# Routing three of the four groups of tokens: one comparison and the splitting of the ranks, on VectorE before and on GpSimd after

## The chip, the cores and the metric

The kernel runs on one core of one Trainium2 chip. TensorE (PE, with its weight loads as PEld), VectorE (DVE), ScalarE (ACT), GpSimd (POOL) and SyncE (SP, which only issues DMAs here) run instruction queues of their own and wait for each other by semaphores. The metric is the device time of one execution in microseconds, lower is better.

## The reference

Linear attention is followed by a mixture of experts with one expert per token. `x` is the attention's output with one row of 512 values for each of 4608 tokens.

```python
def phi(x):
    proj = np.einsum('bhsd,df->bhsf', x, w_phi)
    proj = proj - np.max(np.abs(proj), axis=-1, keepdims=True)
    return np.concatenate([np.exp(proj), np.exp(-proj)], axis=-1)
q_p, k_p = (phi(q), phi(k))              # batch 8, heads 8, seq 576, dim 64, 128 features
kv = np.einsum('bhsf,bhsd->bhfd', k_p, v)
z = np.sum(k_p, axis=2)
num = np.einsum('bhsf,bhfd->bhsd', q_p, kv)
den = np.einsum('bhsf,bhf->bhs', q_p, z)[..., None] + 1e-06
attn = num / den
# mixture of experts: 8 experts, 512 -> 1024 -> 512
logits = x @ w_gate
expert_idx = np.argmax(logits, axis=1)
gate_w = softmax(logits)[np.arange(N), expert_idx]
for e in range(E):
    mask = expert_idx == e
    out[mask] = gate_w[mask, None] * (np.maximum(x[mask] @ w1[e], 0.0) @ w2[e])
```

## The kernel before

The attention works in 16 units: 4 groups of two batches, and in each group 4 pairs of heads. A unit takes its tokens in 9 chunks of 128. Products in fp32 are made from a high and a low part: ScalarE rounds (`xh`, `kh`, `vh`) and GpSimd or VectorE subtracts (`xl`, `kl`, `vl`). The steps of a unit are: `project` (three matmuls for each chunk into `ps_proj`, then VectorE's largest magnitude `mx` and the difference `t`), `k_features` and `k_parts` (exponentials `e`, then `kh` and `kl`), `q_features` (four transposes `pt` of `t`, then exponentials `qp`), the products `pk` of keys and values, `pf` (the folding with `w_gate`), and `pn`, which `normalize` turns into attention rows `xrow` and logits `lgc` (VectorE's `rec`, `rec`, `xrow`, `lgc`). `merge`, `zipped` and `ordered` weave the projections of one unit between the products of the last. `ps_proj` and `pt` have two buffers each, so that VectorE must have made `t` from one `ps_proj` before TensorE may use that buffer again, and TensorE's transposes wait for `t`.

The routing of a group (`route`) runs during the first unit pairs of the next group. Its steps are put between the products one at a time by `spread`. For the first three groups `final` is None, and there `X`, the engine of the small element-wise steps, is GpSimd. `logits`, `top` and `first_top` reduce on VectorE; `shift` and `candidates` are GpSimd's. `one_hot` compares the expert's number with each token's choice (`oh_b`), copies it to fp32 (`onehot`), and `sum_up` counts (`gsum` on VectorE, added to `base`). After some steps of pause, `count_ranks` counts with matmuls (`prk`) the place of each token among its expert's, `rank` reduces it to one number for each token, `rank_parts` splits it into a block of 128 and the place in it, and `rank_values` writes these as fp32, `blk` and `rkr`. Then `select` makes for each of 9 chunks one 128x128 table on VectorE (`sel_p`) and one on GpSimd (`sel_h`), and `gate`, `gate_sum`, `gate_store` make the gate weights (`se`, `gt`). The fourth group (`final` given) is routed at the end of the attention, with all of it on VectorE. The third pass is followed by `lead`, which fetches the first rows for the experts.

A scheduler sets the order on each engine from the order of the calls and from its own estimate of times, so that an edit in one step can move others. Each engine works strictly in that order. A wait of VectorE holds up all that stands behind it.

Of the kernel before, what the change touches and what calls it, by code (L numbers as in the profile page):

```python
# [14 lines left out]
ALU = mybir.AluOpType  # L15
AX = mybir.AxisListType
# [3 lines left out]
P = 128  # L20
# [8 lines left out]
NC = 9  # L29
# [12 lines left out]
W = 73  # L42
XW = DM + 4
BIG = 8192.0


@with_exitstack
def tile_linear_attention_moe(
# [12 lines left out]
    V, A, G, T = nc.vector, nc.scalar, nc.gpsimd, nc.tensor  # L61
# [98 lines left out]
    blk = rt.tile([P, NTILE], F32, name="blk")  # L160
# [410 lines left out]
    def route(g, lgc, c0, n, final=None):  # L571

        j0 = g * NC + c0
        js = slice(j0, j0 + n)
        r = {}
# [3 lines left out]
        X = V if final is not None else G  # L579

        def tile_of(name, shape, dtype=F32, **kw):
            r[name] = sg.tile(shape, dtype, name=name, **kw)[:, 0:n]
            return r[name]
# [22 lines left out]

        def one_hot():
            oh_b = tile_of("oh_b", [P, NC, E], BF16)
            V.tensor_tensor(
                oh_b,  # L610
                iota_em.unsqueeze(1).to_broadcast([P, n, E]),
                choice[:, js].unsqueeze(2).to_broadcast([P, n, E]),
                op=ALU.is_equal,
            )
            X.tensor_copy(onehot[:, js, :], oh_b)
            r["base_b"] = sg.tile([P, E], BF16, name="base_b")
            X.tensor_copy(r["base_b"], base)
# [26 lines left out]
                V.tensor_tensor(tile_of("rks", [P, NC, E]), prk, onehot[:, js, :], op=ALU.mult)  # L644

        def rank():
            with nc.allow_low_precision("ranks are integers"):
                V.tensor_reduce(tile_of("rki", [P, NC], I32), r["rks"], axis=AX.X, op=ALU.add)

        def rank_parts():  # L650
            rkb = tile_of("rkb", [P, NC], I32)
            V.tensor_single_scalar(rkb, r["rki"], 7, op=ALU.arith_shift_right)
            V.tensor_single_scalar(r["rki"], r["rki"], P - 1, op=ALU.bitwise_and)

        def rank_values():
            X.tensor_copy(blk[:, js], r["rkb"])
            X.tensor_copy(tile_of("rkr", [P, NC], bufs=2), r["rki"])

        def select_a(c):

# [27 lines left out]
        steps = [logits, top, shift, candidates, first_top, one_hot]  # L688
        selects = [lambda c=c: select(c) for c in range(n)]
        ranks = [rank, rank_parts, rank_values]  # L690
        gates = [gate, gate_sum, gate_store]
        if final is not None:
# [171 lines left out]
    def tokens_of():  # L864
# [6 lines left out]
        emp = sg.tile([P, NB], F32, name="emp")  # L871
        V.tensor_scalar(emp, pp, 0.5, BIG, op0=ALU.is_lt, op1=ALU.mult)
        V.scalar_tensor_tensor(sidx, pp, -1.0, emp, op0=ALU.add, op1=ALU.add)
# [200 lines left out]
    op = ctx.enter_context(tc.tile_pool(name="op", bufs=2, side="left", reuse_waits="tile"))  # L1074
# [142 lines left out]
```

## Time and profile before

| | |
|---|---|
| median of 3 runs | 940.46 us (940.34 to 940.65) |
| profiled execution, its own time | 942.13 us |
| its span in the profile | 940.1 us |
| TensorE, matmuls | busy 900.6 us, 96% |
| VectorE | busy 591.0 us, 63% |
| ScalarE | busy 591.9 us, 63% |
| GpSimd | busy 499.4 us, 53% |
| mean granted TensorE clock | 0.986 |

The span runs from the first to the last instruction in the profile; 2.0 us lie around it. Busy shares are averages over the whole span. The attention ends near 438 us and the experts fill the rest. The three routing passes that the change touches run near 134 to 162, 236 to 264 and 339 to 367 us.

### The profile page before, as it was taken

The numbers are of one execution on the slowest core, as the hardware profiler recorded it, in microseconds if no ns is written. First come the engines' busy times: TensorE is split into PE (matmuls) and PEld (weight loads), VectorE is DVE, ScalarE is ACT, GpSimd is POOL, SyncE is SP. The second block draws the span as 40 slices with busy tenths as digits, with TensorE's granted clock in tenths as the row PEclk, the third lists the DMA queues.
The fourth block names the chain that finished last, engine by engine and source line by source line (L and its number), as shares of the span: only waits on it lengthen the run. The fifth ranks groups of instructions, "written<-read, shape, count | busy, mean of one in ns | idle before, by whom it ended". The sixth has DMA issues, their size and how long they took to land. (4 is left out here: it accounts for less than half of the span.)

```text
span 940.1 us, 18395 instructions
## 1 busy us (share of the span) xinstructions
PE 900.6 (96%) x6824; PEld 844.2 (90%) x6824; DVE 591.0 (63%) x1016; ACT 591.9 (63%) x895; POOL 499.4 (53%) x355
## 2 busy tenths in 40 slices
PE   6999998999899999999999999999999999999995
PEld 5899998999899989998789999999999999987884
DVE  7767779777887778847864444444444444457850
ACT  5977776777677766654555555555555555568961
POOL 6666668666686669543443333333333333346641
PEclk9999999999999999997999999999999999999998
DMA  4333333333233333143044144441434634764100
GB/s 128 112 98 100 105 105 94 104 93 104 54 89 103 105 105 94 50 141 112 14 136 134 45 144 127 142 128 45 149 115 155 213 117 148 224 204 136 45 24 15
DMA packets 64348, 102.38 MB, mean 109 GB/s; under 512 B 10686, under 2 KB 28478, under 8 KB 64256
## 3 DMA queue, kind: packets, MB, share of 16 engines
q1 hardware_dynamic: 56928, 80.34, 27.6%
q0 software_dynamic: 6720, 20.80, 7.1%
q8 instruction: 54, 0.88, 0.4%
q14 instruction: 38, 0.31, 0.1%
q10 hardware_dynamic: 608, 0.05, 0.0%
HBM read 136.74 MB, written 20.26 MB: 167 GB/s over the span
## 5 line engine op out<-in xcount | busy, mean ns | idle before, releaser
L928 DVE TENSOR_TENSOR wl<-raw,wh 128x1024 fp32r<-128x1024 f32 x137 | 183.6, 1353 | 139.2 <-ACT wh L927 135.7
L927 ACT CAST wh<-raw 128x1024 fp32r<-128x1024 f32 x184 | 191.5, 1050 | 103.3 <-PE po L992 69.2
L928 POOL TENSOR_TENSOR wl<-raw,wh 128x1024 fp32r<-128x1024 f32 x47 | 116.1, 2474 | 178.8 <-ACT wh L927 171.4
L363 PE MATMUL pn<-kf,qp 128*128 128x73 f32 x1024 | 157.2, 256 | 0.0
L971 PE MATMUL pm<-xl,wh 128*128 128x256 f32 x544 | 154.6, 284 | 0.0
L972 PE MATMUL pm<-xh,wl 128*128 128x256 f32 x544 | 154.5, 284 | 0.0
L970 PE MATMUL pm<-xh,wh 128*128 128x256 f32 x544 | 153.9, 283 | 0.0
L363 PEld LDWEIGHTS pn<-kf,qp 128*128 128x128 f32 x1024 | 151.2, 193 | 0.2
L252 DVE TENSOR_REDUCE mx<-ps_proj 128x4 f32<-128x512 f32 (+1 forms) x160 | 100.6, 630 | 67.4 <-PE ps_proj L248 66.9
L275 POOL TENSOR_TENSOR kl<-e,kh 128x1024 fp32r<-128x1024 f32 x47 | 112.1, 2385 | 39.4 <-ACT kh L273 39.4
L235 POOL TENSOR_TENSOR xl<-xr,xh 128x512 fp32r<-128x512 f32 (+2 forms) x62 | 88.0, 1419 | 54.8 <-ACT xh L234 54.5
L990 PE MATMUL po<-wh,hh 128*128 128x512 f32 x272 | 109.3, 402 | 0.0
L991 PE MATMUL po<-wl,hh 128*128 128x512 f32 x272 | 107.3, 395 | 0.4 <-DVE wl L928 0.4
L992 PE MATMUL po<-wh,hl 128*128 128x512 f32 x272 | 106.7, 392 | 0.7 <-DVE hl L978 0.7
L971 PEld LDWEIGHTS pm<-xl,wh 128*128 128x128 f32 x544 | 104.7, 192 | 2.5
L970 PEld LDWEIGHTS pm<-xh,wh 128*128 128x128 f32 x544 | 104.6, 192 | 2.6
L972 PEld LDWEIGHTS pm<-xh,wl 128*128 128x128 f32 x544 | 104.7, 192 | 0.0
L253 DVE TENSOR_TENSOR t<-ps_proj,mx 128x512 f32<-128x512 f32 (+1 forms) x160 | 101.0, 633 | 3.4
L315 PE MATMUL pk<-kh,vl 128*64 128x256 f32 x320 | 98.3, 307 | 2.2 <-POOL vl L303 2.2
L246 PE MATMUL ps_proj<-w_hi,xh 128*128 128x256 f32 x288 | 92.9, 323 | 7.8 <-DVE xh L234 4.3
L315 PE MATMUL pk<-kl,vh 128*65 128x256 f32 x320 | 97.9, 306 | 1.0 <-POOL kl L275 0.7
L315 PE MATMUL pk<-kh,vh 128*65 128x256 f32 x320 | 98.3, 307 | 0.4 <-DVE vh L302 0.4
(217 smaller groups left out, 2029.8 us busy)
## 6 DMA issues: line engine op xcount, KB each, us to landing
raw<-w SPq DMA_DIRECT2D x184, 512.0 KB
vt<-vv SPq DMA_DIRECT2D x16, 640.0 KB
x_dram<-xrow SPq DMA_DIRECT2D x30, 256.0 KB
xr<-kT SPq DMA_DIRECT2D x15, 320.0 KB
xr<-qT SPq DMA_DIRECT2D x15, 320.0 KB
xr<-kT SPq DMA_DIRECT2D x17, 256.0 KB
xr<-qT SPq DMA_DIRECT2D x17, 256.0 KB
x_dram<-xrow SPq DMA_DIRECT2D x32, 32.0 KB
```

Source lines behind the costliest of these rows:

```text
L253: V.tensor_tensor(t[:, 0 : 2 * n, :], psv, mx[:, 0 : 2 * n].unsqueeze(2).to_broadcast([P, 2 * n, F]), op=ALU.subtract,)
L275: eng.tensor_tensor(kl, e[:, 0:m], kh, op=ALU.subtract)
L315: return T.matmul(st["pk", bb][0:n, hh, :], (vl if j == 1 else vh)[:, 2 * (c + (bb if c == 8 else 0)) + hh, 0:n], (kl if j == 2 else kh)[: ...
L363: m = T.matmul(st["pn"][:, 2 * (c % 3) + hh, :], qp[:, s, s0 + hh, :] if c < 8 else qp[:, s, hh, bb : bb + 2].rearrange("p b q -> p (b q)" ...
L927: A.copy(th, raw[k])
L928: (G if k in (POOL_LO if u else POOL_LO0) else V).tensor_tensor(tl, raw[k], th, op=ALU.subtract)
L970: T.matmul(pm[:, i], th, xh[:, k, :], start=(k == 0), stop=False)
L971: T.matmul(pm[:, i], th, xl[:, k, :], start=False, stop=False)
L972: T.matmul(pm[:, i], tl, xh[:, k, :], start=False, stop=(k == KD - 1))
L990: T.matmul(po, hh[:, i, r], th[:, c], start=(i == j == 0), stop=False)
L991: T.matmul(po, hh[:, i, r], tl[:, c], start=False, stop=False)
L992: T.matmul(po, hl[:, i, r], th[:, c], start=False, stop=(i == 1 and j == 3))
```

## The change

In the passes with `final` None, the comparison becomes a subtraction and a test for zero on GpSimd. The ranks stay fp32: the block is found by multiplying by 1/128 and rounding with a large constant that is added and taken off again, the place by taking 128 times the block off the rank. All five of these are GpSimd's. The reduction `rank` stays on VectorE and writes fp32. The fourth group's routing is as before.

```diff
+ROUND = 1.5 * 2.0**23
@@ one_hot
             oh_b = tile_of("oh_b", [P, NC, E], BF16)
-            V.tensor_tensor(
-                oh_b,
+            which = (
                 iota_em.unsqueeze(1).to_broadcast([P, n, E]),
                 choice[:, js].unsqueeze(2).to_broadcast([P, n, E]),
-                op=ALU.is_equal,
             )
+            if final is not None:
+                V.tensor_tensor(oh_b, *which, op=ALU.is_equal)
+            else:
+                G.tensor_tensor(r["cand"], *which, op=ALU.subtract)
+                G.tensor_single_scalar(oh_b, r["cand"], 0.0, op=ALU.is_equal)
@@ rank
+            if final is None:
+                r["rkf"], r["near"] = r["cand"][:, :, 0], r["cand"][:, :, 1]
+                V.tensor_reduce(r["rkf"], r["rks"], axis=AX.X, op=ALU.add)
+                return
             with nc.allow_low_precision("ranks are integers"):
                 V.tensor_reduce(tile_of("rki", [P, NC], I32), r["rks"], axis=AX.X, op=ALU.add)
@@ rank_parts
+            if final is None:
+                near = r["near"]
+                G.tensor_scalar(near, r["rkf"], 1.0 / P, -63.5 / P, op0=ALU.mult, op1=ALU.add)
+                G.tensor_scalar_add(near, near, ROUND)
+                G.tensor_scalar_add(blk[:, js], near, -ROUND)
+                return
             rkb = tile_of("rkb", [P, NC], I32)
             V.tensor_single_scalar(rkb, r["rki"], 7, op=ALU.arith_shift_right)
             V.tensor_single_scalar(r["rki"], r["rki"], P - 1, op=ALU.bitwise_and)
@@ rank_values
-            X.tensor_copy(blk[:, js], r["rkb"])
-            X.tensor_copy(tile_of("rkr", [P, NC], bufs=2), r["rki"])
+            rkr = tile_of("rkr", [P, NC], bufs=2)
+            if final is None:
+                G.tensor_scalar_mul(rkr, blk[:, js], -float(P))
+                G.tensor_tensor(rkr, rkr, r["rkf"], op=ALU.add)
+                return
+            V.tensor_copy(blk[:, js], r["rkb"])
+            V.tensor_copy(rkr, r["rki"])
```

For each of the three passes VectorE loses three instructions and GpSimd gets seven for two. Lines of the changed kernel have numbers that are higher by 2 ahead of these edits and by 22 behind them.

The first place is the counting in the first pass. This is VectorE's order before, from the choice of the expert to the second `t` behind it:

```order
L605 TENSOR_REDUCE choice<-cand 128x9 [waits Pool_49]
L253 TENSOR_TENSOR t<-ps_proj,mx 128x512 [waits DVE_49]
L609 TENSOR_TENSOR oh_b<-iota_em,choice 128x72 [waits DVE_49]
L252 TENSOR_REDUCE mx<-ps_proj 128x4 [waits PE_49]
L630 TENSOR_REDUCE gsum<-onehot 128x8 [waits Pool_49]
L253 TENSOR_TENSOR t<-ps_proj,mx 128x512 [waits DVE_49]
```

This is the same stretch of VectorE in the changed kernel:

```order
L607 TENSOR_REDUCE choice<-cand 128x9 [waits Pool_49]
L255 TENSOR_TENSOR t<-ps_proj,mx 128x512 [waits DVE_49]
L701 TENSOR_REDUCE se<-ex 128x9 [waits Activation_49]
L254 TENSOR_REDUCE mx<-ps_proj 128x4 [waits PE_49]
L636 TENSOR_REDUCE gsum<-onehot 128x8 [waits Pool_49]
L255 TENSOR_TENSOR t<-ps_proj,mx 128x512 [waits DVE_49]
```

And this is GpSimd in that stretch, before:

```order
L602 TENSOR_TENSOR cand<-cand,iota_p 128x72 [waits Pool_49]
L275 TENSOR_TENSOR kl<-e,kh 128x1024 [waits Activation_49]
L615 CAST onehot<-oh_b 128x72 [waits DVE_49]
L631 TENSOR_TENSOR base<-base,gsum 128x8 [waits DVE_49]
L235 TENSOR_TENSOR xl<-xr,xh 128x640 [waits DMAHW7_49,PE_49,Activation_49]
```

and in the changed kernel:

```order
L604 TENSOR_TENSOR cand<-cand,iota_p 128x72 [waits Pool_49]
L277 TENSOR_TENSOR kl<-e,kh 128x1024 [waits Activation_49]
L619 TENSOR_TENSOR cand<-iota_em,choice 128x72 [waits DVE_49]
L620 TENSOR_SCALAR oh_b<-cand 128x72 [waits Pool_49]
L702 TENSOR_SCALAR se<-se 128x9 [waits DVE_49]
L621 CAST onehot<-oh_b 128x72 [waits Pool_49]
L637 TENSOR_TENSOR base<-base,gsum 128x8 [waits DVE_49]
L237 TENSOR_TENSOR xl<-xr,xh 128x640 [waits DMAHW7_49,PE_49,Activation_49]
```

The comparison has left VectorE, which now reduces `se` there. On GpSimd the subtraction, the test and the step `se` stand behind the large `kl` and in front of `onehot`. VectorE's `gsum` still waits for `onehot`, and `t` still stands behind `gsum`.

The second place is the splitting of the ranks in the first pass. VectorE before, from the reduction of the ranks to the first `mx` of the next unit:

```order
L648 TENSOR_REDUCE rki<-rks 128x9 [waits DVE_49]
L252 TENSOR_REDUCE mx<-ps_proj 128x4 [waits PE_49]
L652 TENSOR_SCALAR rkb<-rki 128x9 [waits DVE_49]
L253 TENSOR_TENSOR t<-ps_proj,mx 128x512 [waits DVE_49]
L390 TENSOR_SCALAR rec<-pn 128x6 [waits PE_49]
L653 TENSOR_SCALAR rki<-rki 128x9 [waits DVE_49]
L391 RECIPROCAL rec<-rec 128x6 [waits DVE_49]
L393 TENSOR_TENSOR xrow<-pn,rec 128x384 [waits DVE_49]
L399 TENSOR_TENSOR lgc<-pn,rec 128x3x16
L671 TENSOR_SCALAR sel_p<-iota_pb,rkr,part_133 128x128 [waits Pool_49]
L671 TENSOR_SCALAR sel_p<-iota_pb,rkr,part_133 128x128 x8
L252 TENSOR_REDUCE mx<-ps_proj 128x2 [waits PE_49]
```

VectorE in the changed kernel:

```order
L655 TENSOR_REDUCE cand<-rks 128x9 [waits DVE_49]
L254 TENSOR_REDUCE mx<-ps_proj 128x4 [waits PE_49]
L255 TENSOR_TENSOR t<-ps_proj,mx 128x512 [waits DVE_49]
L392 TENSOR_SCALAR rec<-pn 128x6 [waits PE_49]
L693 TENSOR_SCALAR sel_p<-iota_pb,rkr,part_133 128x128 [waits Pool_49]
L393 RECIPROCAL rec<-rec 128x6 [waits DVE_49]
L693 TENSOR_SCALAR sel_p<-iota_pb,rkr,part_133 128x128
L395 TENSOR_TENSOR xrow<-pn,rec 128x384 [waits DVE_49]
L401 TENSOR_TENSOR lgc<-pn,rec 128x3x16
L693 TENSOR_SCALAR sel_p<-iota_pb,rkr,part_133 128x128 x7
L254 TENSOR_REDUCE mx<-ps_proj 128x2 [waits PE_49]
```

GpSimd there before:

```order
L275 TENSOR_TENSOR kl<-e,kh 128x1024 [waits Activation_49]
L235 TENSOR_TENSOR xl<-xr,xh 128x640 [waits DMAHW1_49,PE_49,Activation_49]
L303 TENSOR_TENSOR vl_158<-vt,vh_156 128x1280 [waits DMAHW0_49,Activation_49]
L617 CAST base_b<-base 128x8 [waits PE_49,Pool_49]
L656 CAST blk<-rkb 128x9 [waits DVE_49]
L235 TENSOR_TENSOR xl<-xr,xh 128x512 [waits DMAHW6_49,PE_49,Activation_49]
L657 CAST rkr<-rki 128x9 [waits DVE_49]
L671 TENSOR_SCALAR sel_h<-iota_pb,rkr,hbase 128x128 [waits Pool_49]
```

and in the changed kernel:

```order
L277 TENSOR_TENSOR kl<-e,kh 128x1024 [waits Activation_49]
L237 TENSOR_TENSOR xl<-xr,xh 128x640 [waits DMAHW1_49,PE_49,Activation_49]
L623 CAST base_b<-base 128x8 [waits PE_49,Pool_49]
L664 TENSOR_SCALAR cand<-cand 128x9 [waits DVE_49]
L305 TENSOR_TENSOR vl_158<-vt,vh_156 128x1280 [waits DMAHW0_49,Activation_49]
L665 TENSOR_SCALAR cand<-cand 128x9 [waits Pool_49]
L666 TENSOR_SCALAR blk<-cand 128x9 [waits Pool_49]
L675 TENSOR_SCALAR rkr<-blk 128x9 [waits Pool_49]
L676 TENSOR_TENSOR rkr<-rkr,cand 128x9 [waits Pool_49]
L693 TENSOR_SCALAR sel_h<-iota_pb,rkr,hbase 128x128 [waits Pool_49]
```

Shift and mask have left VectorE. Four of GpSimd's five new instructions stand behind the large `vl`. The first `sel_p`, which waits for the last of them, has moved up on VectorE, in front of `xrow` and `lgc` and of the next unit's `mx`. The second pass reads the same. In the third, `vl` stands in front of all five, and VectorE makes both `rec` before its first `sel_p`.

## Rows read from the trace of the kernel before

**Rows 1.** The page's first part: busy time, share of the span and number of instructions of each engine.

```profile
PE 900.6 (96%) x6824; PEld 844.2 (90%) x6824; DVE 591.0 (63%) x1016; ACT 591.9 (63%) x895; POOL 499.4 (53%) x355
```

**Rows 2.** Busy time in four stretches, the first without routing and the others with one pass each. Columns: from and to (us), length, busy us and instructions of PE, PEld, DVE, ACT and POOL, granted TensorE clock, share of the DMA engines, GB/s.

```profile
108.00:134.00 26.00, 26.00 (x245) 25.99 (x245) 19.02 (x40) 19.47 (x34) 15.30 (x8) 1.00 0.36 109
...
134.00:162.00 28.00, 24.41 (x234) 23.82 (x231) 24.74 (x55) 18.85 (x33) 22.86 (x23) 1.00 0.29 79
236.00:264.00 28.00, 24.45 (x220) 23.86 (x219) 23.49 (x53) 18.56 (x31) 21.47 (x22) 0.94 0.29 78
339.00:367.00 28.00, 24.40 (x232) 23.80 (x231) 25.24 (x57) 18.52 (x32) 22.40 (x22) 1.00 0.31 83
```

**Rows 3.** Timeline of TensorE in the three passes, the instructions that it came to late. Columns: start (us), duration, engine, line, operation, output from inputs, shape, count, and in brackets the idle time before it and what ended that.

```profile
139.86 0.36 PE L246 MATMUL ps_proj<-w_hi,xh 128*128 128x256 f32 x1 [0.61 <-DVE t L253]
142.82 0.63 PE L284 MATMUL pt<-ident,t 128*128 128x128 f32 x4 [1.43 <-DVE t L253]
154.34 0.66 PE L284 MATMUL pt<-ident,t 128*128 128x128 f32 x4 [1.55 <-DVE t L253]
...
244.76 1.09 PE L284 MATMUL pt<-ident,t 128*128 128x128 f32 x4 [1.44 <-DVE t L253]
257.69 0.66 PE L284 MATMUL pt<-ident,t 128*128 128x128 f32 x4 [1.51 <-DVE t L253]
...
348.12 0.63 PE L284 MATMUL pt<-ident,t 128*128 128x128 f32 x4 [1.42 <-DVE t L253]
359.67 0.66 PE L284 MATMUL pt<-ident,t 128*128 128x128 f32 x4 [1.56 <-DVE t L253]
```

**Rows 4.** Timeline of VectorE in the first pass, the counting.

```profile
139.63 1.66 DVE L609 TENSOR_TENSOR oh_b<-iota_em,choice 128x72 bf16<-128x72 f32 x1
141.21 0.68 DVE L252 TENSOR_REDUCE mx<-ps_proj 128x4 f32<-128x512 f32 x1
141.81 0.27 DVE L630 TENSOR_REDUCE gsum<-onehot 128x8 f32<-128x72 f32 x1
142.00 0.67 DVE L253 TENSOR_TENSOR t<-ps_proj,mx 128x512 f32<-128x512 f32 x1
```

**Rows 5.** Timeline of GpSimd in the first pass.

```profile
138.81 2.38 POOL L275 TENSOR_TENSOR kl<-e,kh 128x1024 fp32r<-128x1024 f32 x1
141.35 0.24 POOL L615 CAST onehot<-oh_b 128x72 f32<-128x72 bf16 x1 [0.16 <-DVE oh_b L609]
...
143.94 1.31 POOL L680 TENSOR_SCALAR se<-se 128x9 f32<-128x9 f32 x1
...
147.12 2.39 POOL L275 TENSOR_TENSOR kl<-e,kh 128x1024 fp32r<-128x1024 f32 x1 [0.85 <-ACT kh L273]
149.47 1.56 POOL L235 TENSOR_TENSOR xl<-xr,xh 128x640 fp32r<-128x640 f32 x1
150.98 2.68 POOL L303 TENSOR_TENSOR vl<-vt,vh 128x1280 fp32r<-128x1280 f32 x1
153.61 0.19 POOL L617 CAST base_b<-base 128x8 bf16<-128x8 f32 x1
```

**Rows 6.** Groups of GpSimd's small instructions, all of the span. Columns: line, engine, operation, output from inputs, shapes, count, then busy us in total and mean ns of one, then idle time before them and what ended it.

```profile
L601 POOL TENSOR_SCALAR cand<-lg 128x72 f32<-128x72 f32 x3 | 1.4, 467 | 0.3
L602 POOL TENSOR_TENSOR cand<-cand,iota_p 128x72 f32<-128x72 f32 x3 | 1.0, 337 | 0.0
...
L631 POOL TENSOR_TENSOR base<-base,gsum 128x8 f32<-128x8 f32 x3 | 0.6, 204 | 1.7 <-DVE gsum L630 1.7
...
L142 POOL TENSOR_SCALAR iota_em<-iota_p 128x8 f32<-128x8 f32 x1 | 0.3, 258 | 0.1
```

**Rows 7.** Timeline of VectorE in the first pass, from a `kl` of its own to the next unit's first `t`.

```profile
143.93 1.20 DVE L275 TENSOR_TENSOR kl<-e,kh 128x1024 fp32r<-128x1024 f32 x1
...
151.34 2.35 DVE L652 TENSOR_SCALAR rkb<-rki 128x9 int32<-128x9 int32 x1
153.61 0.68 DVE L253 TENSOR_TENSOR t<-ps_proj,mx 128x512 f32<-128x512 f32 x1
...
155.12 0.18 DVE L391 RECIPROCAL rec<-rec 128x6 f32<-128x6 f32 x1
...
155.92 2.30 DVE L671 TENSOR_SCALAR sel_p<-iota_pb,rkr,part 128x128 bf16<-128x128 bf16 x9
158.01 0.41 DVE L252 TENSOR_REDUCE mx<-ps_proj 128x2 f32<-128x256 f32 x1
...
159.16 0.17 DVE L390 TENSOR_SCALAR rec<-pn 128x6 f32<-128x6 f32 x1 [0.21 <-PE pn L363]
...
160.48 0.42 DVE L253 TENSOR_TENSOR t<-ps_proj,mx 128x256 f32<-128x256 f32 x1
```

**Rows 8.** Timeline of TensorE behind the first pass: the transposes that wait for the `t` of 160.48.

```profile
161.18 0.38 PE L284 MATMUL pt<-ident,t 128*128 128x128 f32 x2
```

**Rows 9.** Timeline of TensorE between the attention and the experts, its two longest waits there.

```profile
429.28 0.66 PE L950 MATMUL px<-ident,xg 128*128 128x128 f32 x2 [2.33 <-issue]
...
458.47 0.18 PE L868 MATMUL pp<-bsel,sel_p 128*128 128x43 bf16 x1 [1.71 <-DVE bsel L857]
```

**Rows 10.** Busy time and granted clock in the 3 us behind each of these two waits, columns as in rows 2.

```profile
429.30:432.30 3.00, 3.00 (x15) 3.00 (x16) 3.00 (x6) 0.00 (x0) 1.50 (x1) 0.50 0.00 0
...
458.50:461.50 3.00, 3.00 (x74) 2.90 (x74) 1.64 (x5) 1.85 (x2) 0.12 (x1) 0.65 0.01 3
```

## The prediction, made before the changed kernel had run

> **What bounds the kernel now.** I read the page's first part, then stretches of the attention side by side, then what TensorE waited for in the three passes that the change touches. TensorE is busy for 96% of the span and no other engine for more than 63% [rows 1]. In a stretch without routing it is busy without a gap. A stretch with a pass costs it about 3.6 us of idle time, 24.4 busy of 28 [rows 2]. All of it lies at three places of a pass, and each time TensorE waited for VectorE's `t`: 0.61, 1.43 and 1.55 us in the first pass, and almost the same in the others [rows 3]. So an edit of the routing is worth what it does to these waits, and to the new ones that it may bring. Nothing else in the pass is on the path that sets the end.
>
> The second wait comes from the comparison. VectorE starts `oh_b` at 139.63 and is done at 141.29, 1.66 us for 72 elements; GpSimd's `kl` ran from 138.81 to 141.19 [rows 4, 5]. Behind `oh_b` stand `mx`, `gsum` and the late `t` of 142.00. The third comes from the shift: `rkb` took 2.35 us and `t` came at 153.61, when `vl` on GpSimd had run from 150.98 to 153.66 [rows 5, 7].
>
> **What the change removes.** Comparison, shift and mask leave VectorE. If nothing took their place, the second and third wait would go, 2.98 us a pass or 8.9 us in all. What takes their place is read from the order and priced below, for the first pass.
>
> **The counting.** `gsum` still waits for GpSimd's `onehot`, and `t` stands behind `gsum`. GpSimd now has four instructions behind `kl`. The next instruction starts about 0.04 ahead of the end of the last where it need not wait (147.12 + 2.39 against 149.47), and about 0.06 behind what it waits for (`oh_b` ends at 141.29, `onehot` starts at 141.35) [rows 4, 5]. So the subtraction starts at 141.15; at the 0.34 of the other two-input step on 72 elements it ends at 141.49. The test for zero has no row. Its bounds are 0.26 (one step on 8 elements) and 0.47 (two steps on 72) [rows 6]; I take 0.45 for the like number of elements, and it ends at 142.00. The step `se` took 1.31 where it stood, beside a `kl` of VectorE's of 143.93 to 145.13 [rows 5, 7]. Now VectorE idles there, waiting for `onehot`, so I take 0.26 [rows 6], to 142.22. `onehot` takes 0.24, to 142.42, and `gsum` starts at 142.48 where it started at 141.81 [rows 4]. `t` is 0.7 us later than before and the second wait grows from 1.43 to 2.1 us. With the lowest prices (0.26 and 0.20) it is 0.4 later, with the highest (0.47 and 1.31) 1.7.
>
> **The third wait.** `mx` is followed by `t` at once, at 151.34 + 0.7 = 152.0, done at 152.7. TensorE, 0.7 late itself, comes to the transposes at 154.34 - 1.55 + 0.7 = 153.5 [rows 3, 7]. This wait goes whole. At this point TensorE is 1.55 - 0.7 = 0.85 us ahead of before.
>
> **The ranks.** Now VectorE's first `sel_p` waits for the last of GpSimd's five instructions. Behind it stand one `rec`, `xrow`, `lgc`, eight `sel_p` and the next unit's `mx` and `t`; TensorE waits for these. GpSimd is 0.7 late from its `kl` of 147.12 on, which waits for ScalarE, which follows TensorE [rows 5]. So `xl` ends at 151.73, `base_b` at 151.88, and the first of the five at 152.12 at a price of 0.28 (bounds 0.26 to 0.47 [rows 6]). `vl` comes next, from 152.08 to 154.76, 1.1 us later than before. Then three single steps at 0.26 and one two-input step at 0.20 [rows 6], each 0.06 behind the last: 154.72 + 1.16 = 155.88. `sel_p` starts at 155.94. Before, VectorE needed 2.89 us from `rec` at 155.12 to `mx` at 158.01 for these same instructions [rows 7]. Now `mx` starts at 155.94 + 2.89 = 158.83, 0.82 late. Of this the idle 0.21 ahead of the `rec` of 159.16 gives back its part, and the `t` of 160.48 is 0.61 late. The transposes that need it stood at 161.18, 0.28 behind its end; the shortest such step is 0.15 (142.67 to 142.82) [rows 3, 4, 7, 8], so 0.13 was spare. TensorE leaves the pass 0.48 us later than before, for all that it was 0.85 ahead in the middle.
>
> The second pass has the same order. In the third `vl` stands ahead of all five and one `rec` ahead of `sel_p`, which moves the result by some 0.2. With the lowest prices throughout (0.4 in the counting, 0.20 for each small step) a pass costs nothing; with the highest (1.7, and 0.47 for each step) 2.4 us. I take 0.5, near the rows of like size, so 1.5 us for three passes.
>
> A rule speaks for more. GpSimd's `kl` of 1024 elements takes 2.38 where VectorE's takes 1.20 [rows 5, 7], and the Trainium skill, GPSIMD Engine Reference, section "Performance versus the Vector engine", says that ordinary element-wise arithmetic does not belong on GpSimd, VectorE being about twice as fast. An estimate by that page, with twice VectorE's 0.18 of a small step for each of the last four, gives a `sel_p` about 0.4 later, and a total 1.2 us above mine. The row of GpSimd's own small step is nearer, and the sum stays with it.
>
> **The clock.** Behind the wait of 1.44 in the second pass the granted clock fell from its upper level of 2.4 GHz to 1.2 for a while: four transposes took 1.09 us where they take 0.63, and the mean clock there is 0.94 against 1.00 [rows 2, 3]. From that place to the third wait's end the second pass needed 12.93 us (244.76 to 257.69), the first 11.52 and the third 11.55, so a fall costs 1.4. Of the six waits of 1.42 to 1.56, one was followed by a fall; of the two longer ones behind the attention, 1.71 and 2.33, both were [rows 9, 10]. The wait of 2.1 lies between those two. I count 2.5 falls in three passes for the one before: 1.5 more, 2.1 us.
>
> **The sum.** 1.5 + 2.1 = 3.6 us. The profiled execution took 942.13 us and would take 945.7; it stands 1.7 above the median of the runs, so against that median, 940.46, the forecast is 944.1. Its own range is 942.4 to 946.5.
>
> **The rivals.** About 0.2%, 1.9 us, is what a measurement of this kernel can tell from no change.
> - *The clock falls no oftener than before.* The wait of 2.1 is only a third longer than waits that passed without a fall. Then 940.46 + 1.5 = 942.0, the same within the bound. Chance 0.25.
> - *The ranks come in time.* If GpSimd's last steps are hidden, TensorE keeps its 0.85 us a pass: 937.9, or about 940 with one or two falls more. It decides where `sel_p` starts: ahead of 155.46 a pass gains, at 154.6 it gains all. For it speaks that GpSimd's spans are rough; against it, that `vl` alone ends at 154.76. Chance 0.1, half of it faster.
> - *Both waits go and no new one comes,* if `onehot` and the ranks are there when VectorE comes to them: 931.5. The four instructions behind `kl` speak against it. Chance 0.04.
> - *GpSimd's small steps are held up by VectorE.* `se` started at 143.94 and took 1.31 us, ending 0.12 behind VectorE's `kl` [rows 5, 7]. If one step in the counting is held up like this, each pass costs 1.05 more: 944.1 + 3.2 = 947.3. It needs a `kl` of VectorE's in that place, and the order shows none. Chance 0.12. The Trainium skill, SBUF — State Buffer, section "SBUF: two separate sides", has the mechanism: the port pair that the two engines share is an exclusive lock for a whole instruction. The trace agrees, by the 0.12.
>
> **The chances.** The forecast has 0.49. Faster takes 0.04 and half of the 0.1: 0.09. The same takes the other half and 0.25: 0.30. Slower takes 0.49 + 0.12: 0.61. The range reaches down to 940.0, where ranks in time meet more falls, and up to 947.0, short of the held-up steps; it leaves out about 0.09 below and 0.09 above.
>
> **What would show it.** Right: in the changed profile TensorE's second wait of a pass is about 2.1 us and ends with a `t` behind a `gsum` that waited about 2 us for GpSimd's `onehot`; no wait stands where the third was; VectorE idles about 3 us ahead of the first `sel_p`; new waits of 0.5 to 1 us for the next unit's `t` follow, at the projections and the transposes behind the pass; the granted clock falls in two or three passes. Wrong: a second wait no longer than 1.5 us, or `sel_p` without idle time ahead of it, or no waits behind the pass. A GpSimd step of 9 elements at over 0.5 us would mean that I priced it too low.

## The result and the profile after

The changed kernel took 948.92 us, median of 4 runs (948.43 to 949.35), against 940.48 for the kernel before on the same chip: ratio 1.009, with a 95% interval of 1.0074 to 1.0106. It is 8.4 us slower; 3.6 were forecast. Its profiled execution took 948.91 us, with a span of 947.2. Two executions that stood far from all others, one of run 10 (2251.97 us) and one of the kernel before beside it (1248.79), are left out of the medians and intervals below.

The page's first part, as in [rows 1]:

```profile
PE 905.2 (96%) x6824; PEld 846.7 (89%) x6824; DVE 581.0 (61%) x1007; ACT 591.4 (62%) x895; POOL 502.1 (53%) x370
```

VectorE has lost 10 us and GpSimd got 3, and TensorE, with the same 6824 products, is 4.6 us busier. Most of that is the clock, as below.

TensorE's timeline after, as in [rows 3] and [rows 8]: the products that it came to late, in the three passes, and last the first transposes for the experts.

```profile
138.49 0.36 PE L248 MATMUL ps_proj<-w_hi,xh 128*128 128x256 f32 x1 [0.61 <-DVE se L701]
142.29 1.08 PE L286 MATMUL pt<-ident,t 128*128 128x128 f32 x4 [2.27 <-DVE t L255]
...
159.96 0.38 PE L248 MATMUL ps_proj<-w_hi,xh 128*128 128x256 f32 x1 [0.45 <-DVE t L255]
161.47 0.44 PE L286 MATMUL pt<-ident,t 128*128 128x128 f32 x2 [0.24 <-DVE t L255]
...
165.37 0.33 PE L317 MATMUL pk<-kl,vh 128*65 128x256 f32 x1 [0.15 <-POOL kl L277]
...
242.98 0.36 PE L248 MATMUL ps_proj<-w_hi,xh 128*128 128x256 f32 x1 [0.59 <-DVE se L701]
246.77 0.63 PE L286 MATMUL pt<-ident,t 128*128 128x128 f32 x4 [2.26 <-DVE t L255]
...
347.56 0.36 PE L248 MATMUL ps_proj<-w_hi,xh 128*128 128x256 f32 x1 [0.60 <-DVE se L701]
351.35 1.08 PE L286 MATMUL pt<-ident,t 128*128 128x128 f32 x4 [2.27 <-DVE t L255]
...
370.78 0.38 PE L248 MATMUL ps_proj<-w_hi,xh 128*128 128x256 f32 x1 [1.14 <-DVE t L255]
...
375.23 0.44 PE L365 MATMUL pn<-kf,qp 128*128 128x73 f32 x2 [0.70 <-DVE kf L353]
...
436.11 0.66 PE L972 MATMUL px<-ident,xg 128*128 128x128 f32 x2 [2.33 <-issue]
```

The second wait is there in each pass, longer: 2.27, 2.26, 2.27 for 1.43, 1.44, 1.42. The third is gone. New are the small waits behind the pass, for the next unit's `t` (0.45 and 0.24; 1.14 in the third), for GpSimd's `kl` (0.15) and, in the third pass, for VectorE's `kf` (0.70).

The wait of 0.6 that opens each pass is in both kernels, so it marks the passes. Before, the first stands at 139.86 [rows 3] and the other two here:

```profile
241.79 0.36 PE L246 MATMUL ps_proj<-w_hi,xh 128*128 128x256 f32 x1 [0.59 <-DVE t L253]
345.17 0.36 PE L246 MATMUL ps_proj<-w_hi,xh 128*128 128x256 f32 x1 [0.62 <-DVE t L253]
```

From mark to mark the first pass took 101.93 us and takes 104.49 (+2.56), the second 103.38 and 104.58 (+1.20). The third, up to the transposes of 429.28 [rows 9] and 436.11, took 84.11 and takes 88.55 (+4.44). That is 8.20 in all. The span differs by less, 7.1: the first mark comes 1.37 sooner, since the profiled execution of before had a half-clock stretch ahead of it that this one lacks.

How much of it is clock, the granted clock tells (third figure from the end). These are the 10 us round the second wait of each pass, after:

```profile
138.00:148.00 10.00, 7.24 (x52) 7.10 (x53) 7.17 (x16) 6.48 (x11) 4.89 (x9) 0.83 0.26 56
242.00:252.00 10.00, 7.15 (x49) 6.81 (x49) 6.89 (x17) 6.04 (x11) 5.33 (x8) 0.83 0.26 54
347.00:357.00 10.00, 7.17 (x41) 7.03 (x42) 6.55 (x16) 5.59 (x10) 4.91 (x8) 0.66 0.26 57
```

Before, only the second of the three had a fall, by which this text means a stretch at the lower level of the clock:

```profile
242.00:252.00 10.00, 8.56 (x66) 8.39 (x66) 8.48 (x18) 7.65 (x12) 6.11 (x7) 0.83 0.21 49
```

A mean of 0.83 is a loss of 0.17 x 10 = 1.7 us and 0.66 one of 3.4: 6.8 in all after, 1.7 before. So at most 5.1 of the 8.20 are clock. Part of the loss fell while TensorE was waiting anyway and cost nothing. This is the second wait of the third pass after:

```profile
349.08:351.35 2.27, 0.00 (x1) 0.03 (x1) 1.02 (x3) 1.08 (x2) 1.63 (x6) 0.71 0.00 0
```

That is 0.29 x 2.27 = 0.66 us. The second waits of the first two passes stood at 0.90 and 1.00, which gives 0.23 and 0, and that of the second pass before at 0.86, 0.20. Without these, the clock cost TensorE 5.9 us after and 1.5 before. So some 4.4 of the 8.20 are clock, and 3.8 are waiting: 1.1, 1.0 and 1.7 in the three passes.

The waits in brackets show less than that, since they count from the end of the product's row ahead, and the rows overlap: three `pk` of 0.28 us start at 173.63, 173.75 and 173.86. Product for product, against the kernel before, TensorE fell back by 0.65, 0.41 and 0.31 us at the first pass's new waits of 0.45, 0.24 and 0.15.

### The profile page after: what moved, and what is told of

Read it like the earlier page. It is cut to its first block, busy times and chain, and to the rows that moved or that the text cites. A ratio compares the mean times of both kernels' runs of the same rounds, so it can differ in the third digit from the quotient of the medians.

```text
span 947.2 us, 18405 instructions
## 1 busy us (share of the span) xinstructions
PE 905.2 (96%) x6824; PEld 846.7 (89%) x6824; DVE 581.0 (61%) x1007; ACT 591.4 (62%) x895; POOL 502.1 (53%) x370
## 5 line engine op out<-in xcount | busy, mean ns | idle before, releaser
L949 ACT CAST wh<-raw 128x1024 fp32r<-128x1024 f32 x184 | 191.5, 1050 | 103.4 <-PE po L1014 69.2
L254 DVE TENSOR_REDUCE mx<-ps_proj 128x4 f32<-128x512 f32 (+1 forms) x160 | 100.5, 630 | 69.4 <-PE ps_proj L250 69.1
L993 PEld LDWEIGHTS pm<-xl,wh 128*128 128x128 f32 x544 | 104.7, 192 | 2.5
L992 PEld LDWEIGHTS pm<-xh,wh 128*128 128x128 f32 x544 | 104.5, 192 | 2.6
L994 PEld LDWEIGHTS pm<-xh,wl 128*128 128x128 f32 x544 | 104.7, 192 | 0.0
```

The lines of the kernel that those rows point to most:

```text
L949: A.copy(th, raw[k])
L992: T.matmul(pm[:, i], th, xh[:, k, :], start=(k == 0), stop=False)
L993: T.matmul(pm[:, i], th, xl[:, k, :], start=False, stop=False)
L994: T.matmul(pm[:, i], tl, xh[:, k, :], start=False, stop=(k == KD - 1))
```

## The experiments

Twelve kernels ran beside the kernel before. In the table, the passes are measured from mark to mark as above, the clock is the mean granted clock of 132 to 180, 234 to 282 and 336 to 384 us (rounded, so that 0.01 is 0.48 us of such a window), and the last column has TensorE's longest wait that begins in each of these windows. Each profile is of one execution; each ratio is to executions of the kernel before beside it.

| kernel | median us | ratio to before, 95% | passes, us | clock | longest wait, us |
|---|---|---|---|---|---|
| before | 940.5 | | 101.9, 103.4, 84.1 | 1.00 .96 1.00 | 1.55, 1.51, 1.56 |
| after | 948.9 | 1.0074 to 1.0106 | 104.5, 104.6, 88.6 | .96 .96 .93 | 2.27, 2.26, 2.27 |
| 1 comparison alone | 949.8 | 1.0070 to 1.0134 | 105.2, 106.1, 88.0 | .93 .93 .93 | 2.30, 2.29, 2.26 |
| 2 ranks alone | 951.1 | 1.0086 to 1.0144 | 107.9, 104.7, 88.7 | .89 1.00 .93 | 3.24, 3.22, 3.17 |
| 3 sum behind | 951.2 | 1.0086 to 1.0144 | 105.7, 105.7, 88.1 | .93 .93 .93 | 3.81, 3.80, 3.83 |
| 4 selections behind | 957.4 | 1.0151 to 1.0211 | 107.9, 106.3, 92.6 | .96 .96 .96 | 2.27, 2.27, 4.40 |
| 5 sum behind, order held | 940.6 | 0.9974 to 1.0011 | 102.2, 102.2, 86.9 | .96 .96 .93 | 1.15, 1.12, 2.77 |
| 6 ranks alone, order held | 939.8 | 0.9969 to 1.0009 | 102.3, 102.3, 84.6 | 1.00 1.00 1.00 | 1.42, 1.44, 1.42 |
| 7 before, VectorE's order | 937.2 | 0.9943 to 0.9979 | 101.2, 101.2, 83.2 | 1.00 1.00 1.00 | 0.61, 0.60, 0.62 |
| 8 three `sel_h` on VectorE | 952.2 | 1.0061 to 1.0138 | 105.6, 104.5, 92.5 | .93 .96 .89 | 2.29, 2.26, 2.61 |
| 9 as 6, comparison behind | 940.0 | 0.9978 to 1.0003 | 101.9, 102.0, 84.2 | 1.00 1.00 1.00 | 1.11, 1.13, 0.62 |
| 10 longer second wait | 949.6 | 1.0049 to 1.0104 | 105.8, 105.9, 88.1 | .93 .93 .93 | 1.86, 1.90, 1.88 |
| 11 as 7, `rkr` ahead of `xl` | 934.3 | 0.9915 to 0.9955 | 100.4, 100.5, 82.3 | 1.00 1.00 1.00 | 0.62, 0.60, 0.62 |
| 12 as 5, `vl` behind the ranks | 935.9 | 0.9941 to 0.9978 | 100.8, 101.3, 83.8 | 1.00 1.00 1.00 | 1.25, 0.94, 0.61 |

The edits use one helper: an edge that sets only the order of two instructions of one engine, without a wait. `pin(m, "t", i)` puts `m` behind the i-th `t`, counted from 0 at the start of a pass's routing: 2 is the `t` of the second wait, 6 that of the third. `behind(m)` puts it behind the `t` emitted last. The edits are shown cut to the lines that matter.

### The two halves (1 and 2)

Run 1 is the changed kernel with `rank`, `rank_parts` and `rank_values` as before, run 2 with `one_hot` as before, and `sel_p` behind a `t`:

```diff
@@ select, run 2
-                eng.tensor_scalar(dst[:, j0 + c, :], iota_pb, ...)
+                m = eng.tensor_scalar(dst[:, j0 + c, :], iota_pb, ...)
+                if eng is V and final is None:
+                    behind(m)
```

> Only the comparison goes to GpSimd; shift and mask of the ranks stay on VectorE. Theory W (the second wait of each pass, 2.27 us instead of 1.43, does most of the harm, by itself and through the clock's falls behind it): second waits 2.2 to 2.3 us, third waits 1.4 to 1.6 us still there, so about 0.85 us a pass more than before and more half-clock stretches in the three passes than before's one; 945 to 950 us. Rival L (GpSimd's lag from the steps of the ranks does it): the second wait alone costs 3 x 0.85 us, 941 to 944 us.

> Only the ranks' shift and mask go to GpSimd; the comparison stays on VectorE, and the sel_p are held behind the unit's t as they stand in the changed kernel. Theory W: second waits 1.4 to 1.5 us as before, no third wait, the two small waits behind sel_p (0.45 and 0.24 us) come: 0.8 us a pass less than before and no further half-clock stretch; 936 to 940 us. Rival L: GpSimd ends the pass 1 us or more later, product pk and VectorE's kl wait for it, and the passes lose what the changed kernel loses less 0.85 us each; 943 to 947 us.

Run 1 came out as theory W has it: 949.8 us, second waits of 2.26 to 2.30, third waits of 1.14 to 1.73. Run 2 was a miss for both. Its second wait and its missing third are as W said, but the scheduler had put all nine `sel_h` ahead of GpSimd's next `kl`. GpSimd and TensorE in the first pass:

```profile
155.28 7.23 POOL L698 TENSOR_SCALAR sel_h<-iota_pb,rkr,hbase 128x128 bf16<-128x128 bf16 x9
162.48 1.26 POOL L237 TENSOR_TENSOR xl<-xr,xh 128x512 fp32r<-128x512 f32 x1
163.70 2.34 POOL L287 TENSOR_TENSOR kl<-e,kh 128x1024 fp32r<-128x1024 f32 x1
...
166.09 0.48 PE L327 MATMUL pk<-kl,vh 128*65 128x256 f32 x1 [3.24 <-POOL kl L287]
```

In the kernel before, `kl` stands behind four `sel_h`, at 158.92. Here it came 4.8 us later, and `pk` waited 3.24. So each half alone is as slow as both together, by different waits.

### Taking the second wait away (3, 5, 12)

```diff
@@ sum_up
-                V.tensor_reduce(gsum, ...)
+                m = V.tensor_reduce(gsum, ...)
+                if final is None:
+                    behind(m)
@@ gate_store
-            V.reciprocal(r["se"], r["se"])
+            m = V.reciprocal(r["se"], r["se"])
+            if final is None:
+                behind(m)
```

> The changed kernel, with VectorE's sum over the one-hots (gsum) and the reciprocal of se ordered behind the t of the last unit emitted, so that VectorE waits for GpSimd's comparison only when the pass's t are through. Theory W: the second wait (2.27 us) falls under 0.5 us in each pass and the half-clock stretches behind it go; 3 x 2 us and some 4 us of clock less than the changed kernel, 936 to 941 us. Rival L: the second wait goes, but what hangs on the sum or on GpSimd's row comes later by as much, 943 to 947 us.

951.2 us, a miss. The second wait went, but with less ahead of it a `sel_p` slipped ahead of a `t`. VectorE and TensorE in the first pass:

```profile
152.50 0.31 DVE L705 TENSOR_SCALAR sel_p<-iota_pb,rkr,part 128x128 bf16<-128x128 bf16 x1 [4.38 <-POOL rkr L688]
152.73 0.68 DVE L265 TENSOR_TENSOR t<-ps_proj,mx 128x512 f32<-128x512 f32 x1
...
153.47 1.12 PE L296 MATMUL pt<-ident,t 128*128 128x128 f32 x4 [3.81 <-DVE t L265]
```

VectorE stood 4.38 us before `sel_p` with `t` behind it. In run 5 both are pinned behind `t` 3, and `sel_p` and `sel_h` are held where the changed kernel has them:

```diff
@@ select
+                if eng is V:
+                    pin(m, "t", 6)
+                if eng is G and c >= 6:
+                    pin(m, "kl", 2)
```

> The changed kernel, with the sum over the one-hots (gsum) and the reciprocal of se behind the third t after the top of the ranking is known, and the rest of both engines' orders (sel_p, sel_h) held as in the changed kernel, which the third run did not do. Theory W (each wait of TensorE above 1.4 us costs its length and often a stretch at half clock): the second wait of 2.27 us falls under 0.3 us in each pass, no 3.8 us wait takes its place, 6.8 us less and up to 5 us of clock less than the changed kernel: 934 to 940 us. Rival L (GpSimd's lag behind the pass): TensorE comes to pk 2 us earlier and waits there for GpSimd's kl instead; 943 to 949 us.

The next unit's `mx` is held behind the last `sel_p` as well, here and in runs 6, 7, 9, 11 and 12. 940.6 us: the whole change, without its second wait, is 8 us faster and level with the kernel before, 0.6 above W's range. The part of W on the clock failed: 0.96, 0.96 and 0.93 is what the change has, so the 6.4 us by which the three passes are shorter are waiting and not clock. What is left in the first two passes are the waits behind `sel_p`. That of 2.77 in the third is another: VectorE's `base_b`, beside GpSimd's `vl`, took 2.58 us and held up `t`. TensorE in the first and third pass, then VectorE and GpSimd in the third:

```profile
156.24 0.39 PE L274 MATMUL ps_proj<-w_hi,xh 128*128 128x256 f32 x1 [1.15 <-DVE t L284]
...
356.50 1.11 PE L318 MATMUL pt<-ident,t 128*128 128x128 f32 x4 [2.77 <-DVE t L284]
...
352.41 2.58 DVE L660 CAST base_b<-base 128x8 bf16<-128x8 f32 x1
...
355.75 0.69 DVE L284 TENSOR_TENSOR t<-ps_proj,mx 128x512 f32<-128x512 f32 x1
...
352.27 2.70 POOL L337 TENSOR_TENSOR vl<-vt,vh 128x1280 fp32r<-128x1280 f32 x1
```

Run 12 moves `vl` behind the five steps among which it stood. `count` numbers the instructions of a kind, `name` gives one a name, and `ahead` puts the `vl` behind the one that is named:

```diff
@@ v_parts
-        G.tensor_tensor(vl, ...)
+        count(G.tensor_tensor(vl, ...), "vl")
@@ rank_values
-                G.tensor_tensor(rkr, rkr, r["rkf"], op=ALU.add)
+                name(G.tensor_tensor(rkr, rkr, r["rkf"], op=ALU.add), ("rkr", g))
+                ahead["vl", count_of["vl"]] = [("rkr", g)]
```

> The fifth run (the whole change, the sum over the one-hots behind later t's) with GpSimd's large vl behind the five steps of the ranks, which it stood among. Theory W: sel_p starts 1 to 2 us sooner, the waits of 1.15 and 0.24 us (2.77 in the third pass) and the half-clock stretches behind them go: 934 to 937 us, so that the change with its waits taken out is no worse than the kernel before with VectorE's order alone. Rival L: GpSimd does the same work and ends the pass as late, pk or VectorE's kl wait for it instead: 939 to 942 us.

935.9 us, in W's range, but only partly for W's reason. In the third pass the wait of 2.77 went, since `base_b`, no longer beside `vl`, took 0.15 us (at 350.88); that of 0.45 behind `sel_p` is the longest left in that window but the mark. In the first the wait stayed, 1.25, since the first `sel_p`, ready 1 us after VectorE came to it, then ran as long as `vl`:

```profile
150.60 2.67 DVE L733 TENSOR_SCALAR sel_p<-iota_pb,rkr,part 128x128 bf16<-128x128 bf16 x1 [1.03 <-POOL rkr L715]
...
150.52 2.70 POOL L338 TENSOR_TENSOR vl<-vt,vh 128x1280 fp32r<-128x1280 f32 x1
```

The clock is 1.00 in all three passes where run 5 had 0.96, 0.96 and 0.93, though waits of 1.1 to 1.3 stand in both. Why they drew a fall there and not here is open.

### The other small terms (4, 6, 8, 9)

> The changed kernel, with every sel_p ordered behind the t of the last unit emitted and the selections emitted one step later, so that VectorE no longer stands 3 us before sel_p with the next unit's work behind it. Theory W: the second wait stays 2.2 to 2.3 us with its half-clock stretches, the waits behind sel_p (0.45 and 0.24 us; 0.31 and 0.25; 1.14 and 0.26) go, 2 to 2.7 us less, 945 to 948 us. Rival L (the wait before sel_p is where GpSimd's lag reaches TensorE): the held kl of VectorE and the waits of pk go with it, 941 to 944 us.

Run 4 has `behind(m)` at `sel_p` as run 2, and the selections one step later. 957.4 us, a miss for both and the slowest of all. The selections no longer stood together, and single ones met GpSimd's long instructions. VectorE, GpSimd and TensorE in the third pass:

```profile
380.25 5.24 DVE L703 TENSOR_SCALAR sel_p<-iota_pb,rkr,part 128x128 bf16<-128x128 bf16 x1
...
380.34 1.29 POOL L237 TENSOR_TENSOR xl<-xr,xh 128x512 fp32r<-128x512 f32 x1
381.58 2.37 POOL L287 TENSOR_TENSOR kl<-e,kh 128x1024 fp32r<-128x1024 f32 x1
383.90 1.54 POOL L237 TENSOR_TENSOR xl<-xr,xh 128x640 fp32r<-128x640 f32 x1
...
386.96 1.09 PE L296 MATMUL pt<-ident,t 128*128 128x128 f32 x4 [4.40 <-DVE t L265]
```

This wait ends behind the third window, whose 0.96 goes with the pass's second wait of 2.27.

> Only the ranks' shift and mask on GpSimd, with the order of sel_p and sel_h held as in the changed kernel, so that no nine sel_h stand before GpSimd's kl. Theory W: the wait of pk for GpSimd's kl, 3.2 us a pass in the second run, falls under 0.5 us; second wait 1.4 us as before, no third wait, small waits of 0.4 to 0.7 us a pass behind sel_p: 937 to 942 us, no slower than before by more than 0.2%. Rival L: GpSimd's five steps alone make it late, pk keeps a wait over 1 us in each pass; 944 to 950 us.

Run 6 is run 2 with `sel_p` and `sel_h` held as in run 5, and 11 us faster: 939.8, no wait of `pk`. The ranks on GpSimd cost nothing in themselves, and gain nothing: the third wait is gone, and waits of 0.61, 0.24 and 0.39 us behind `sel_p` and for `kf` take its place.

```diff
@@ select, run 8
-            for eng, dst, by in ((V, sel_p, part1), (G, sel_h, ...)):
+            for eng, dst, by in ((V, sel_p, part1), (V if final is None and c >= 6 else G, sel_h, ...)):
```

> The changed kernel, with the sel_h of the last three chunks of each pass on VectorE, which takes 2.4 us of work from GpSimd behind the ranks. Rival L: the waits of pk for GpSimd's kl (0.15 to 0.4 us) and the held kl of VectorE (2.27 instead of 1.2 us) go, 0.8 us a pass and what clock hangs on it: 944 to 947 us. Theory W: these are small; VectorE's three more selections ahead of a t give 0.3 us a pass back, the second wait and its half-clock stretches stay: 947 to 950 us.

952.2 us, a miss for both and inconclusive: `pk` no longer waits, but VectorE's three more instructions brought waits of 1.86 and 2.61 in the third pass. Its executions took 946.57 to 952.71.

> The sixth run (ranks' shift and mask on GpSimd, order held) with VectorE's comparison, the sum over the one-hots and the reciprocal of se behind later t's, as in the seventh. Theory W: the second wait of 1.42 us a pass goes too; of the 4.3 us that the sixth run still spends on it, two thirds come back: 935 to 938 us. Rival L: the small waits behind sel_p (0.6, 0.24 and 0.4 us) grow by as much, since the ranks come from GpSimd no sooner: 938.5 to 941 us.

Run 9 is run 6 with `oh_b` behind `t` 2, `gsum` behind 3, the reciprocal behind 4. 940.0 us: rival L's number. The second wait goes, and the first of the small waits grows from 0.61 to 1.11.

### VectorE's order alone (7 and 11)

```diff
@@ the kernel before
+            pin(m, "t", 2)      # m is oh_b
+                pin(m, "t", 3)      # m is gsum
+            pin(m, "t", 6)      # m is rkb
```

> The kernel before, nothing on another engine: VectorE's comparison oh_b stands behind the next t instead of ahead of it, gsum and the reciprocal of se later still, and the shift rkb behind the t that it held up. Theory W (what costs time is what stands ahead of a t, not which engine does it): second wait (1.43 us) and third wait (1.55 us) fall under 0.4 us each in all three passes, 3 x 2.6 us less and no half-clock stretch in the passes: 930 to 935 us. Rival L: GpSimd, not VectorE, sets the pass; the waits turn up at pk or at sel_p, 937 to 942 us.

Here the reciprocal of `se` is behind `t` 4 too, and the order of `sel_h` is held. 937.2 us, faster than before by 0.4%, with neither the second wait nor the third. `oh_b` and `rkb` still take 1.59 and 1.87 us; nothing waits for them there. That is rival L's number, with waits behind `sel_p` as it said; W stood 2 to 7 us too low. Of 2.98 us a pass, 0.7 to 0.9 came back. Most of the rest went into waits behind `sel_p` that the old waits had hidden: 0.43, 0.24 and 0.53 in the first pass, at which TensorE fell back by 1.72 us, product for product. VectorE stood there 0.94 us for `rkr`, which stood behind an `xl` on GpSimd. Run 11 puts `rkr` ahead of it (`xl` 4 is the fifth of GpSimd's from the pass's start):

```diff
@@ rank_values
-            X.tensor_copy(tile_of("rkr", [P, NC], bufs=2), r["rki"])
+            m = X.tensor_copy(tile_of("rkr", [P, NC], bufs=2), r["rki"])
+            if final is None:
+                name(m, ("rkr", g))
+                ahead["xl", r["xl"] + 4] = [("rkr", g)]
```

> The seventh run with one more order: GpSimd writes blk and rkr ahead of the xl that stood before them, so that VectorE's sel_p no longer wait 0.94 us for rkr. Theory W: the small waits behind sel_p (0.43 and 0.24 us in the seventh run) go, 0.7 us a pass: 934 to 936.5 us. Rival L: xl comes 0.4 us later and what GpSimd does behind it too, and the kl of VectorE that stands beside GpSimd's kl keeps its 1.8 us: no change, 936.5 to 938 us.

934.3 us, in W's range and the fastest, 0.65% below before and 14.6 us below the change. The clock is 1.00 in all three windows.

### The wait by itself (10)

```diff
@@ sum_up, the kernel before
-                gsum = sg.tile([P, E], F32, name="gsum")
-                V.tensor_reduce(gsum, onehot[:, js, :].rearrange("p c e -> p e c"), axis=AX.X, op=ALU.add)
+                sums = onehot[:, js, :].rearrange("p c e -> p e c")
+                gsum = r["cand"][:, 0, :]
+                V.tensor_reduce(r["cand"], sums.unsqueeze(1).to_broadcast([P, n, E, n]), axis=AX.X, op=ALU.add)
```

> The kernel before, with the sum over the one-hots done nine times in one instruction of VectorE (about 0.6 us longer), ahead of the same t; all else where it was, but the reciprocal of se, which is held behind the ranks. This lengthens the second wait alone, from 1.43 to 2.0 us. If only its length counts: 3 x 0.6 us, 942 to 943 us, as many half-clock stretches in the passes as before. If a wait of 2 us costs clock as well, as the changed kernel suggests: two or more further half-clock stretches, 944 to 947 us.

The reciprocal of `se` is behind `t` 6 here. 949.6 us, above both ranges. TensorE's second and third wait in the first pass, and the three windows:

```profile
142.71 0.78 PE L316 MATMUL pt<-ident,t 128*128 128x128 f32 x4 [1.86 <-DVE t L282]
155.39 0.66 PE L316 MATMUL pt<-ident,t 128*128 128x128 f32 x4 [1.82 <-DVE t L282]
```

```profile
132.00:180.00 48.00, 43.68 (x380) 43.19 (x380) 38.43 (x78) 33.07 (x56) 33.95 (x32) 0.93 0.25 69
234.00:282.00 48.00, 43.66 (x381) 43.19 (x379) 39.29 (x83) 31.58 (x55) 31.50 (x31) 0.93 0.32 88
336.00:384.00 48.00, 43.64 (x381) 43.16 (x381) 37.00 (x79) 28.97 (x52) 34.06 (x32) 0.93 0.34 97
```

The waits are 0.43 and 0.27 us longer, 0.70 to 0.79 in a pass, and the passes 3.89, 2.49 and 3.96. Of these 10.3 us, 3 x 3.4 - 1.7 = 8.5 are clock: the passes grew by 4.6 times what the waits did. Nothing moved to GpSimd here, and the loss is that of the change. Two limits belong to this: the third wait grew along with the second, and the price is that of one execution, when the others took 943.8 to 950.4 us.

## Why the prediction was wrong

The direction was right (slower, 0.61), the range was not: 948.9 lies above 947.0.

**The counting** held. The subtraction took 0.32 (0.34 taken), the test 0.41 (0.45), `se` 0.26, `onehot` 0.24. GpSimd, then VectorE, in the first pass:

```profile
139.77 0.32 POOL L619 TENSOR_TENSOR cand<-iota_em,choice 128x72 f32<-128x72 f32 x1
140.18 0.41 POOL L620 TENSOR_SCALAR oh_b<-cand 128x72 bf16<-128x72 f32 x1
140.66 0.26 POOL L702 TENSOR_SCALAR se<-se 128x9 f32<-128x9 f32 x1
140.99 0.24 POOL L621 CAST onehot<-oh_b 128x72 f32<-128x72 bf16 x1
...
141.26 0.28 DVE L636 TENSOR_REDUCE gsum<-onehot 128x8 f32<-128x72 f32 x1 [2.19 <-POOL onehot L621]
141.46 0.68 DVE L255 TENSOR_TENSOR t<-ps_proj,mx 128x512 f32<-128x512 f32 x1
```

The second wait was forecast at 2.1 and is 2.27. **The third wait** went, as worked out.

**The ranks** held too: 0.26 for the single steps, 0.21 for the last, and VectorE idle for 3.01 us ahead of `sel_p` ("about 3").

```profile
152.26 2.68 POOL L305 TENSOR_TENSOR vl<-vt,vh 128x1280 fp32r<-128x1280 f32 x1
155.03 0.26 POOL L665 TENSOR_SCALAR cand<-cand 128x9 f32<-128x9 f32 x1
...
156.05 0.21 POOL L676 TENSOR_TENSOR rkr<-rkr,cand 128x9 f32<-128x9 f32 x1
...
156.29 0.32 DVE L693 TENSOR_SCALAR sel_p<-iota_pb,rkr,part 128x128 bf16<-128x128 bf16 x1 [3.01 <-POOL rkr L676]
```

TensorE came to the transposes behind the pass at 161.47, for 161.18 before [rows 8], +0.29; at the pass's opening it was at -1.37. Of the 1.66 between, some 1.5 are clock. So up to this row the pass lost 0.2 us, no more than the 0.48 forecast. In the second and third pass the same transposes stand at 266.01 for 264.52 and at 372.28 for 366.52, and the like reckoning gives 0.1 and 0.6: 0.9 in all, where 1.5 was forecast.

**Where the sum stopped** is the first step that failed: it ended at that row, on the claim that nothing else in the pass is on the path that sets the end. At the next mark the difference is 1.19 (242.98 against 241.79): 0.9 us came in behind it, 0.36 by the late `pk` of 165.37 and 0.5 more by the transposes of 175.74. GpSimd had five `sel_h`, an `xl` and another `sel_h` ahead of its `kl`, where it had four `sel_h`, and was late from there on:

```profile
162.94 2.38 POOL L277 TENSOR_TENSOR kl<-e,kh 128x1024 fp32r<-128x1024 f32 x1
...
171.20 1.55 POOL L237 TENSOR_TENSOR xl<-xr,xh 128x640 fp32r<-128x640 f32 x1
...
171.57 2.27 DVE L277 TENSOR_TENSOR kl<-e,kh 128x1024 fp32r<-128x1024 f32 x1
```

Its `kl` came at 162.94 for 158.92, and `pk` waited. Its `xl` of 171.20 now met VectorE's `kl` of 171.57, which took 2.27 where it had taken 1.22. The second pass lost 0.9 behind the row as well and the third 1.1, 2.9 us in all where the sum has nothing. In the third, VectorE's `kl` met GpSimd's of 371.27 to 373.65, took 1.99 where it had taken 1.13, and held up `kf`, for which TensorE waited 0.70:

```profile
372.23 1.99 DVE L277 TENSOR_TENSOR kl<-e,kh 128x512 fp32r<-128x512 f32 x1
```

In runs 5 and 12, where GpSimd comes to the ranks sooner, no such wait of `pk` is left. That these 2.9 us come of GpSimd's lateness is read from the traces; run 8, which was to remove the term by itself, brought other waits.

**The clock** is the mis-sized term: 2.1 us were forecast, some 4.4 came. In the prediction's terms 2.5 falls at 1.4 us were counted; what came were three, one of them twice as long, and 1.7 us of clock for each single one, 1.5 where part of it fell in a wait. The count of 2.5 lay between six waits of 1.4 to 1.6, one of them followed by a fall, and two of 1.7 and 2.3, both followed. Run 10 speaks for the longer two. Over the profiles of all 14 kernels, the longest wait was 1.8 us or more in 22 passes, and in 21 of them the clock of the window was below 1.00; it was 1.1 to 1.6 in 11, below 1.00 in 3; and under 1.0 in 9, in none. The loss for a pass by these windows was 1.9 to 3.4 us, and 5.3 at most (0.89). Either both waits draw a fall, as in run 10, or one stretch is longer, as in the third pass after (0.66 above). What draws a fall is not settled by this: run 5, which has no wait of 2.27, lost as much clock as the change.

With the terms at their measured size (0.9 up to the row and 2.9 behind it for 1.5, 4.4 for 2.1) the sum is 8.2, as the passes from mark to mark have it, and 8.4 is what the runs gave. *The clock falls no oftener* is refuted by the windows, *both waits go* by the rows of TensorE, *the ranks come in time* by VectorE's 3.01 us ahead of `sel_p`. *Small steps held up by VectorE* did not occur: none of the steps that are new on GpSimd took over 0.41.

## What to carry to other kernels

Where the bound engine waits at the head of a pass, cost a longer wait with the clock that it can draw, and take the price from a run that lengthens the wait and moves nothing, in more than one execution. Follow a late engine past the row where the sum ends, up to the next place at which both kernels stand alike. Before work is given to another engine, try it where it is, behind the instruction that it holds up: order alone gave 0.65%, and moving the work with a poor order cost 0.9%.

## What was not expected of the hardware

One `sel_p` of VectorE, 128 elements and mostly 0.31 us in the kernel before, took 5.24 us in run 4, from 380.25 to 385.49. It began in the last 0.12 us of GpSimd's `sel_h` of 377.95, and GpSimd then ran an `xl`, a `kl` and an `xl` without a gap until 385.44. The Trainium skill, SBUF — State Buffer, section "Who interferes with whom", says that issue order decides which of the two blocks and that the port pair is held for a whole instruction. The row agrees on the blocking; that VectorE was not let in between three GpSimd instructions goes further than the page.

A mean clock below 1.00 round a pass did not follow from a wait's length alone: one wait of 3.22 us (run 2, second pass) left it at 1.00, and two of 1.15 and 1.12 (run 5) did not.
